# Two-layer feed-forward kernel on TensorE: y operands of layer 2 prepared for two pairs at once, 1024 columns wide

## The chip, the cores and the metric

The kernel runs on one core of a Trainium2 chip. The metric is the time of one execution on the device in microseconds (us), of which the median over several runs is compared.

## The reference

Three stages follow each other on the same 3072 tokens (4 batches x 768):

```python
x = attention(q, k, v, mem_k, mem_v)       # chunked, 8 heads of 64, to (3072, 512)
h = x @ w_in;  x = (h - tanh(h)) @ w_out   # layer 1: 512 -> 2048 -> 512
h = x @ w_in2                              # layer 2: 512 -> 2048
g = maximum(h, 0) + alpha * minimum(h, 0)
out = g @ w_out2                           # y: 2048 -> 512
```

The change touches layer 2 alone.

## The kernel before, in words

Each fp32 operand of a matmul is held as a rounded part (hi) and the rest (lo); a product of two such operands is three matmuls, hi hi, hi lo and lo hi (the table `PASS`). ScalarE (ACT) makes hi by a copy into the rounded type, and VectorE (DVE) or GpSimd (POOL) makes lo = value - hi.

Layer 2 takes both its matmuls in the form with seven block products in place of eight. It goes through the tokens in NB = 3 blocks of 1024 (two halves of 512 columns), and through the 2048 inner channels in P2 = 8 pairs of 256 (two tiles of 128). A block has two stages:

- `pair_h` computes the inner activations of a pair: seven products of six matmuls (L408), numbered 1 to 7, sums of them on DVE (L425, with ACT copies `hs`, `hv`), and `prelu` (ACT L416, L417, DVE L418). It leaves four tiles of 128 x 512: `ga0`, `ga1`, `gb0`, `gb1`, which lie in the pair's `gx` = (ga0, gb1) and `gy` = (ga1, gb0). POOL then makes t3 = gb1 - ga1 (L459) and, in place, ga1 = ga1 - ga0 (L460).
- the y stage goes through the seven products in the order `ORDER` = 1, 6, 5, 2, 7, 3, 4, each a phase of 8 pairs. For a pair, `prep` makes the operand (hi and lo in one tile `go`) and `y_product` issues six matmuls (L502), three for each of two output tiles `yb` in PSUM, which sum over the pairs. `y_done` (L509, L520) combines the products, and L532 turns the result for the store.

The operand of product 1 is ga0, of 5 ga1, of 2 gb0, of 7 t3, of 3 gb1. Product 6 takes t3 + ga0, which L478 writes into a PSUM bank of its own; L481 rounds it, L483 splits it, and L485 puts gb0 minus it over ga0, which is the operand of product 4.

In the main loop `prep` runs LEAD = 6 pairs ahead of `y_product`; EARLY = 4 of them are issued ahead of the block's last pair. Which engine splits: POOL for product 1 from the third pair on, and for every fourth pair of products 5, 2, 7, 3, 4; DVE otherwise. The last pair of a block, the y stage and the first products of the next block are one stream on PE: a scheduler of the Tile framework sets the order on each engine from its own estimate of times, and `issue_after` only moves a piece's priority. In phases 2 to 6, `load_x2`, `sum_x2` (L384) and `split_x2` (L121 on ACT, L122 on POOL) prepare the next block's inputs. SP issues all loads: `wi` (input weights, L370) and `wo` (output weights, L362). The pool `w` of 34 buffers holds `gx`, `gy`, `go` and the weights.

Of the kernel before, what the change touches and what calls it, by code (L numbers as in the profile page):

```python
# [7 lines left out]
FP32 = mybir.dt.float32  # L8
FP32R = mybir.dt.float32r
U32 = mybir.dt.uint32  # L10
U64 = mybir.dt.uint64
ACTF = mybir.ActivationFunctionType
ALU = mybir.AluOpType
# [24 lines left out]
def chunk_attention_two_ffn_kernel(  # L38
# [12 lines left out]
    nc = tc.nc  # L51
# [14 lines left out]
    def f32(ap):  # L66
        return ap.bitcast(FP32)

    const = ctx.enter_context(tc.tile_pool(name="const", bufs=1))
    w_p = ctx.enter_context(tc.tile_pool(name="w", bufs=2 * NF + 2))  # L70
# [274 lines left out]
    P2 = NF // 2  # L345
    NB = NTILE // 8
    NO = 7 * P2 // 2
    LEAD = 6
    EARLY = 4
    wo2 = {}  # L350
    win = {}
    xop = {}
    xin = {}
    gx = {}
    gy = {}
    t3 = {}
    gop = {}

# [42 lines left out]
    def product(h, i, m, first):  # L401
        b = i // P2
        s = WSLOT[m]
        w, x = win[i, s // 2][:, :, s % 2], xop[b, m]
        j = 0
        for kt in range(2):
            for a, c in PASS:
                nc.tensor.matmul(  # L408
                    out=h, lhsT=w[:, a, 128 * kt:128 * kt + 128], rhs=x[c][:, kt, :],
                    start=(first and j == 0), stop=(j == 5), skip_group_check=True,  # L410
                )
                j += 1

    def prelu(t, h, f):
        n = t_p.tile([128, 512], FP32, tag="t", name="n")
        nc.scalar.activation(out=n, in_=h, func=ACTF.Relu, scale=-1.0)  # L416
        nc.scalar.activation(out=n, in_=n, func=ACTF.Copy, scale=alpha_neg[:, f:f + 1])  # L417
        last["pre"] = nc.vector.scalar_tensor_tensor(  # L418
            out=t, in0=h, scalar=0.0, in1=n, op0=ALU.max, op1=ALU.add
        ).ins  # L420

    def pair_h(i):
        b, p = divmod(i, P2)
        f = 2 * p
        add = lambda o, p, q: nc.vector.tensor_tensor(out=o, in0=p, in1=q, op=ALU.add)  # L425
        d = {}
        x = gx[b, p] = w_p.tile([128, 2, 512], FP32, tag="w", name="gx")
        y = gy[b, p] = w_p.tile([128, 2, 512], FP32, tag="w", name="gy")
        if p % 2 == 0:
            t3[b, p // 2] = zr.tile([128, 2, 512], FP32, tag="t3", name="t3")  # L430
        d3 = t3[b, p // 2][:, p % 2]
        ga, gb = (x[:, 0], y[:, 0]), (y[:, 1], x[:, 1])

        for m in (1, 6, 5, 7) if p % 2 else (6, 1, 5, 7):
            if b % 2:
                d[m] = ps_y.tile([128, 512], FP32, tag="y", name="h2")
            elif m in (1, 6):
                d[m] = ps_h.tile([128, 512], FP32, tag="h", name="h2")
            else:
                d[m] = ps_h2.tile([128, 512], FP32, tag="h2", name="h2")  # L440
        product(d[1], i, 1, True)
        hs = g_p.tile([128, 512], FP32, tag="gh", name="hs")
        nc.scalar.activation(out=hs, in_=d[1], func=ACTF.Copy)
        product(d[6], i, 6, True)
        hu = g_p.tile([128, 512], FP32, tag="gl", name="hu")
        add(hu, d[6], hs)
        product(d[5], i, 5, True)
        add(d[5], d[5], hu)
        hv = g_p.tile([128, 512], FP32, tag="gh", name="hv")
        nc.scalar.activation(out=hv, in_=d[5], func=ACTF.Copy)  # L450
        product(d[7], i, 7, True)
        add(gb[1], d[7], hv)
        add(d[7], d[7], hu)
        prelu(gb[1], gb[1], f + 1)
        product(d[1], i, 2, False)
        prelu(ga[0], d[1], f)
        product(d[5], i, 3, False)
        prelu(ga[1], d[5], f)
        nc.gpsimd.tensor_tensor(out=d3, in0=gb[1], in1=ga[1], op=ALU.subtract)  # L459
        nc.gpsimd.tensor_tensor(out=ga[1], in0=ga[1], in1=ga[0], op=ALU.subtract)  # L460
        product(d[7], i, 4, False)
        prelu(gb[0], d[7], f + 1)

    def y_bank(b, m):
        if (b % 2 == 0) == (m in (1, 6)):
            return ps_y.tile([128, 512], FP32, tag="y", name="yb")
        if m in (1, 5):
            return ps_h.tile([128, 512], FP32, tag="h", name="yb")
        return ps_h2.tile([128, 512], FP32, tag="h2", name="yb")

    def prep(b, s):
        mi, p = divmod(s, P2)
        m = ORDER[mi]
        x, y, d3 = gx[b, p], gy[b, p], t3[b, p // 2][:, p % 2]
        op = w_p.tile([128, 2, 512], FP32R, tag="w", name="go")
        if m == 6:
            src = y_bank(b, 7)
            nc.vector.tensor_tensor(out=src, in0=d3, in1=x[:, 0], op=ALU.add)  # L478
        else:
            src = {1: x[:, 0], 5: y[:, 0], 2: y[:, 1], 7: d3, 3: x[:, 1], 4: x[:, 0]}[m]  # L480
        nc.scalar.activation(out=op[:, 0], in_=src, func=ACTF.Copy)  # L481
        eng = nc.gpsimd if (m == 1 and p > 1) or (m not in (1, 6) and p % 4 == 3) else nc.vector
        eng.tensor_tensor(out=op[:, 1], in0=src, in1=f32(op[:, 0]), op=ALU.subtract)  # L483
        if m == 6:
            nc.vector.tensor_tensor(out=x[:, 0], in0=y[:, 1], in1=src, op=ALU.subtract)  # L485
        gop[b, s] = op

    yd = {}
    ye = {}

    def y_product(b, s, tiles=(0, 1)):
        mi, p = divmod(s, P2)
        m = ORDER[mi]
        into = {2: 1, 3: 5, 4: 7}.get(m, m)
        if m == into and p == 0 and 0 in tiles:
            yd[b, m] = [y_bank(b, m) for _ in range(2)]
        w = wo2[b * NO + mi * (P2 // 2) + p // 2][:, p % 2]
        w = w.rearrange("k a (i n) -> k a i n", i=2)
        op = gop[b, s]
        for i in tiles:  # L500
            for n, (a, c) in enumerate(PASS):
                nc.tensor.matmul(  # L502
                    out=yd[b, into][i], lhsT=w[:, a, i], rhs=op[:, c],
                    start=(m == into and p == 0 and n == 0), stop=(p == P2 - 1 and n == 2),
                    skip_group_check=True,
                )
# [224 lines left out]
    if True:  # L731
# [8 lines left out]
        def more_w():  # L740
# [10 lines left out]
            out=ident, in_=ident, compare_op=ALU.not_equal, fill=1.0, base=0,  # L751
# [39 lines left out]
        g = 1e9  # L791
        for t in reversed(range(n0 + 2, NTILE + 1)):
            g = min(base[first_of[t - 1][0]] - 3, g - (per(g) if t < NTILE else 0))
# [3 lines left out]
        for t in range(n0 + 1, NTILE + 1):  # L797
            if t == n0 + 1:
                pos = 2
            else:  # L800
                lo = max(pos + SPACE, release(t - 1))
# [5 lines left out]
        for t in range(n0 + 1, NTILE + 1):  # L807
            a, nxt = at[t], at.get(t + 1, 1e9)
# [15 lines left out]
        for i, (l, b, n, f) in enumerate(slots):  # L824
# [13 lines left out]
            if b == N1 - 1:  # L838
                if f == 0:
                    astack.close()  # L840
                    with tc.issue_after(last["dve"]):
                        nc.vector.tensor_scalar(
                            out=alpha_neg, in0=alpha_sb, scalar1=-1.0, scalar2=None, op0=ALU.mult
# [26 lines left out]
        for b in range(NB):  # L870
            more = b + 1 < NB
            for p in range(P2):
                i = b * P2 + p
                if p == P2 - 1:
                    for s in range(EARLY):
                        prep(b, s)
                if i > 0:
                    pair_h(i)
                for q in range(4):
                    win.pop((i, q))  # L880
                if p + 2 < P2:
                    for q in range(4):
                        load_in(i + 2, q)
            early, late = [], []
            if more:
                work = x2_work(b + 1)
                early, late = work[:8], work[8:]
                late[3:3] = [lambda q=q: load_in((b + 1) * P2, q) for q in range(4)]
                late += [lambda q=q: load_in((b + 1) * P2 + 1, q) for q in range(4)]
            with tc.issue_after(last["pre"]):  # L890
                for s in range(EARLY, LEAD):
                    prep(b, s)
            for s in range(7 * P2):
                if s + LEAD < 7 * P2:
                    with tc.issue_after(last["pre"]):
                        prep(b, s + LEAD)
                if more or s < 6 * P2:
                    y_product(b, s)
                    if s % P2 == P2 - 1:
                        y_done(b, ORDER[s // P2])  # L900
                    i = b * NO + s // 2 + 4
                    if s % 2 and i < NB * NO:
                        load_out(i)
                if s >= 2 * P2 and s % 2 == 0 and early:
                    early.pop(0)()
                if s >= 4 * P2 and late:
                    late.pop(0)()
            if not more:
                for i in range(2):
                    for p in range(P2):  # L910
                        y_product(b, 6 * P2 + p, (i,))
                    y_done(b, 4, (i,))
# [61 lines left out]
```

## Time and profile before

| what | value |
|---|---|
| three runs | 1093.62 us median (1093.38 to 1095.15) |
| profiled execution, its own time | 1096.97 us |
| its span, first to last instruction | 1094.1 us |
| mean granted TensorE clock | 0.992 of full |
| PE, DVE, ACT, POOL busy | 97%, 62%, 49%, 42% |
| matmuls | 6912, of them 1008 at L502 and 1008 at L408 |

Layer 2 begins at about 560 us of the span. Its three y stages begin at about 691, 848 and 1006 us. Line numbers in the rows are those of the kernel before; those of the changed kernel are one or three lines off: L417 there is L418 here, L424 is L425, L458 and L459 are L459 and L460, and L476, L478, L482, L485 are the new lines of `prep`.

### The profile page before, as it was taken

How to read it: one execution, taken by the hardware profiler on the slowest of the kernel's cores; microseconds unless marked ns; L12 is line 12 of the kernel's file. 1: busy time of each engine (PE TensorE's matmuls, PEld its weight loads, DVE VectorE, ACT ScalarE, POOL GpSimd, SP SyncE). 2: the span in 40 equal slices, each digit the busy share in tenths (PEclk: the TensorE clock that was granted, in tenths of full speed). 3: DMA queues.
4: the chain of work that ended last, by engine and by line, in shares of the span. 5: the costliest groups of instructions: out<-in, count | busy, mean ns of one | idle time of the engine just before them, and what ended most of it. 6: DMA issues, size and time to landing. Idle time of an engine off the chain costs nothing. (4 is left out here: it accounts for less than half of the span.)

```text
span 1094.1 us, 18216 instructions
## 1 busy us (share of the span) xinstructions
PE 1056.4 (97%) x6912; PEld 863.4 (79%) x6912; DVE 677.7 (62%) x1087; ACT 535.2 (49%) x956; POOL 464.3 (42%) x351
## 2 busy tenths in 40 slices
PE   4599999999999999999999999999999899999998
PEld 4478878888888888888888888878888688888786
DVE  3688855665776566576321255799555898456873
ACT  3466644444445444454342355655356564465650
POOL 3166634444454453445382122528222467124440
PEclk9699999999999999999999999999999999999999
DMA  9773143554555464454711355488844588833576
GB/s 269 276 259 127 59 145 123 203 168 168 179 184 181 156 204 164 174 174 150 221 32 36 145 176 199 131 265 271 259 170 148 181 248 277 244 135 138 153 213 170
DMA packets 99366, 196.22 MB, mean 179 GB/s; under 512 B 36560, under 2 KB 50896, under 8 KB 99280
## 3 DMA queue, kind: packets, MB, share of 16 engines
q1 hardware_dynamic: 93712, 188.52, 52.6%
q10 hardware_dynamic: 5568, 6.56, 1.7%
q8 instruction: 54, 0.88, 0.3%
q14 instruction: 32, 0.26, 0.1%
HBM read 153.10 MB, written 41.94 MB: 178 GB/s over the span
## 5 line engine op out<-in xcount | busy, mean ns | idle before, releaser
L274 PE MATMUL h<-ring,wt 128*128 128x512 f32 x1152 | 282.6, 393 | 5.9 <-ACT ring L681 2.4
L274 PEld LDWEIGHTS h<-ring,wt 128*128 128x128 f32 x1152 | 217.2, 189 | 52.7 <-ACT ring L681 2.6
L502 PE MATMUL yb<-go,wo 128*128 128x512 f32 x1008 | 235.5, 392 | 5.8 <-DVE go L483 2.7
L502 PEld LDWEIGHTS yb<-go,wo 128*128 128x128 f32 x1008 | 187.9, 188 | 51.1 <-DVE go L483 5.3
L408 PE MATMUL h<-xh,wi 128*128 128x512 f32 x672 | 212.1, 391 | 0.7 <-DVE gx L418 0.4
L299 POOL TENSOR_TENSOR gl<-t,gh 128x512 fp32r<-128x512 f32 x96 | 127.0, 1325 | 173.3 <-ACT gh L298 150.6
L313 PE MATMUL y<-gh,wt 128*128 128x512 f32 x768 | 192.8, 392 | 0.0
L313 PEld LDWEIGHTS y<-gh,wt 128*128 128x128 f32 x768 | 143.2, 188 | 30.4
L290 DVE TENSOR_TENSOR t<-h,t 128x512 f32<-128x512 f32 x96 | 65.9, 687 | 140.8 <-ACT t L289 140.6
L408 PEld LDWEIGHTS h<-xh,wi 128*128 128x128 f32 x672 | 126.2, 188 | 30.6 <-ACT hv L450 2.9
L289 ACT ACTIVATE t<-h 128x512 f32<-128x512 f32 x96 | 56.8, 592 | 112.2 <-PE h L274 92.8
L459 POOL TENSOR_TENSOR t<-gx,gy 128x512 f32<-128x512 f32 x24 | 31.1, 1295 | 175.1 <-DVE gy L418 175.1
L313 PE MATMUL y<-gl,wt 128*128 128x512 f32 x384 | 104.3, 390 | 0.0
L298 ACT ACTIVATE gh<-t 128x512 fp32r<-128x512 f32 x96 | 60.4, 629 | 54.2 <-DVE t L290 47.7
L313 PEld LDWEIGHTS y<-gl,wt 128*128 128x128 f32 x384 | 72.0, 188 | 15.0
L408 PE MATMUL h<-xl,wi 128*128 128x512 f32 x192 | 74.8, 390 | 0.0
L122 POOL TENSOR_TENSOR ws<-sm,ws 128x512 fp32r<-128x512 f32 x32 | 42.8, 1338 | 56.9 <-ACT ws L121 41.4
L417 ACT ACTIVATE n<-n,alpha_neg 128x512 f32<-128x512 f32 x96 | 65.9, 719 | 0.6
L122 POOL TENSOR_TENSOR wt<-s,wt 128x512 fp32r<-128x512 f32 x32 | 41.3, 1294 | 41.0 <-ACT wt L121 39.3
L483 DVE TENSOR_TENSOR go<-gx,go 128x512 fp32r<-128x512 f32 x42 | 57.3, 1406 | 1.4 <-ACT go L481 1.4
L408 PE MATMUL h<-x,wi 128*128 128x512 f32 x144 | 56.1, 390 | 0.0
L483 POOL TENSOR_TENSOR go<-gx,go 128x512 fp32r<-128x512 f32 x30 | 44.0, 1479 | 20.0 <-ACT go L481 20.0
(95 smaller groups left out, 1364.5 us busy)
## 6 DMA issues: line engine op xcount, KB each, us to landing
wo<-w2o SPq DMA_DIRECT2D x84, 512.0 KB, 4.2
wi<-w2i SPq DMA_DIRECT2D x72, 512.0 KB, 4.9
kn<-in_k_dram SPq DMA_DIRECT2D x24, 384.0 KB, 4.5
vn<-in_v_dram SPq DMA_DIRECT2D x24, 384.0 KB, 3.8
ri<-in_moe_w_in_dram SPq DMA_DIRECT2D x16, 512.0 KB, 7.7
ro<-in_moe_w_out_dram SPq DMA_DIRECT2D x16, 512.0 KB, 8.5
pk<-in_moe_w_in_dram SPq DMA_DIRECT2D x16, 512.0 KB, 4.0
pk<-in_moe_w_out_dram SPq DMA_DIRECT2D x16, 512.0 KB, 4.1
```

The lines of the kernel that those rows point to most:

```text
L122: nc.gpsimd.tensor_tensor(out=lo, in0=v, in1=f32(hi), op=ALU.subtract)
L274: last["ffn"] = nc.tensor.matmul(out=h, lhsT=wi[:, a, kk, :], rhs=ring[c][:, s0:s0 + n, kk, :], start=(i == 0), stop=(i == 3 * KD - 1),).ins
L289: nc.scalar.activation(out=t, in_=h, func=ACTF.Tanh)
L290: last["dve"] = nc.vector.tensor_tensor(out=t, in0=h, in1=t, op=ALU.subtract).ins
L298: nc.scalar.activation(out=gh, in_=t, func=ACTF.Copy)
L299: nc.gpsimd.tensor_tensor(out=gl, in0=t, in1=f32(gh), op=ALU.subtract)
L313: mm = nc.tensor.matmul(out=yp[l, b][j][:, :n * 128], lhsT=wo[:, a, j * 128:(j + 1) * 128], rhs=g[c], start=first, stop=final,)
L408: nc.tensor.matmul(out=h, lhsT=w[:, a, 128 * kt:128 * kt + 128], rhs=x[c][:, kt, :], start=(first and j == 0), stop=(j == 5), skip_group_c ...
L417: nc.scalar.activation(out=n, in_=n, func=ACTF.Copy, scale=alpha_neg[:, f:f + 1])
L459: nc.gpsimd.tensor_tensor(out=d3, in0=gb[1], in1=ga[1], op=ALU.subtract)
L483: eng.tensor_tensor(out=op[:, 1], in0=src, in1=f32(op[:, 0]), op=ALU.subtract)
L502: nc.tensor.matmul(out=yd[b, into][i], lhsT=w[:, a, i], rhs=op[:, c], start=(m == into and p == 0 and n == 0), stop=(p == P2 - 1 and n == ...
```

## The change

- The four activations become four tiles of 128 x 2 x 512, one for each two pairs (`gq`), in place of `gx` and `gy` of each pair.
- `prep` works on two pairs at once: one rounding and one split, each 1024 columns, into two tiles, `goh` and `gol`.
- The sum for product 6 is made in place in SBUF over ga0 (L476), not in a PSUM bank; the operand of product 4 is made in place over gb0 (L478), in product 4's own phase, not in product 6's.
- LEAD and EARLY are counted in double pairs: 3 and 2.
- POOL splits product 1 for three of four double pairs, and the last double pair of the other products in the last block only.

The number of matmuls and what they multiply stay the same.

```diff
     P2 = NF // 2
     NB = NTILE // 8
     NO = 7 * P2 // 2
-    LEAD = 6
-    EARLY = 4
+    LEAD = 3
+    EARLY = 2
...
-        x = gx[b, p] = w_p.tile([128, 2, 512], FP32, tag="w", name="gx")
-        y = gy[b, p] = w_p.tile([128, 2, 512], FP32, tag="w", name="gy")
         if p % 2 == 0:
+            for n in ("ga0", "ga1", "gb0", "gb1"):
+                gq[b, n, p // 2] = w_p.tile([128, 2, 512], FP32, tag="w", name=n)
             t3[b, p // 2] = zr.tile([128, 2, 512], FP32, tag="t3", name="t3")
         d3 = t3[b, p // 2][:, p % 2]
-        ga, gb = (x[:, 0], y[:, 0]), (y[:, 1], x[:, 1])
+        ga, gb = [[gq[b, f"g{r}{k}", p // 2][:, p % 2] for k in range(2)] for r in "ab"]
...
     def prep(b, s):
-        mi, p = divmod(s, P2)
+        mi, pp = divmod(s, P2 // 2)
         m = ORDER[mi]
-        x, y, d3 = gx[b, p], gy[b, p], t3[b, p // 2][:, p % 2]
-        op = w_p.tile([128, 2, 512], FP32R, tag="w", name="go")
+        ga0, ga1, gb0, gb1 = [gq[b, n, pp] for n in ("ga0", "ga1", "gb0", "gb1")]
+        d3 = t3[b, pp]
         if m == 6:
-            src = y_bank(b, 7)
-            nc.vector.tensor_tensor(out=src, in0=d3, in1=x[:, 0], op=ALU.add)
-        else:
-            src = {1: x[:, 0], 5: y[:, 0], 2: y[:, 1], 7: d3, 3: x[:, 1], 4: x[:, 0]}[m]
-        nc.scalar.activation(out=op[:, 0], in_=src, func=ACTF.Copy)
-        eng = nc.gpsimd if (m == 1 and p > 1) or (m not in (1, 6) and p % 4 == 3) else nc.vector
-        eng.tensor_tensor(out=op[:, 1], in0=src, in1=f32(op[:, 0]), op=ALU.subtract)
-        if m == 6:
-            nc.vector.tensor_tensor(out=x[:, 0], in0=y[:, 1], in1=src, op=ALU.subtract)
-        gop[b, s] = op
+            nc.vector.tensor_tensor(out=ga0, in0=d3, in1=ga0, op=ALU.add)
+        if m == 4:
+            nc.vector.tensor_tensor(out=gb0, in0=gb0, in1=ga0, op=ALU.subtract)
+        src = {1: ga0, 6: ga0, 5: ga1, 2: gb0, 7: d3, 3: gb1, 4: gb0}[m]
+        hi = w_p.tile([128, 2, 512], FP32R, tag="w", name="goh")
+        lo = w_p.tile([128, 2, 512], FP32R, tag="w", name="gol")
+        nc.scalar.activation(out=hi, in_=src, func=ACTF.Copy)
+        pool = pp > 0 if m == 1 else b == NB - 1 and pp == 3
+        eng = nc.gpsimd if pool else nc.vector
+        eng.tensor_tensor(out=lo, in0=src, in1=f32(hi), op=ALU.subtract)
+        gop[b, s] = hi, lo
...
-        op = gop[b, s]
+        op = gop[b, s // 2]
...
-                    out=yd[b, into][i], lhsT=w[:, a, i], rhs=op[:, c],
+                    out=yd[b, into][i], lhsT=w[:, a, i], rhs=op[c][:, p % 2],
...
-                if s + LEAD < 7 * P2:
+                if s % 2 == 0 and s // 2 + LEAD < NO:
                     with tc.issue_after(last["pre"]):
-                        prep(b, s + LEAD)
+                        prep(b, s // 2 + LEAD)
```

The change moves instructions on DVE and POOL where a block's y stage begins. DVE in the kernel before, from the activations of the block's last pair (L418) to the second double pair of product 6 in block 0; `t_6408` and `t_6606` are t3 of the first two double pairs, `yb` the PSUM bank:

```order
L418 SCALAR_TENSOR_TENSOR gx<-gx,n 128x512
L418 SCALAR_TENSOR_TENSOR gx<-h_7028,n 128x512
L418 SCALAR_TENSOR_TENSOR gy<-h_7030,n 128x512
L418 SCALAR_TENSOR_TENSOR gy<-h_7031,n 128x512
L478 TENSOR_TENSOR yb<-t_6408,gx 128x512 x2
L483 TENSOR_TENSOR go<-yb,go 128x512
L485 TENSOR_TENSOR gx<-gy,yb 128x512
L483 TENSOR_TENSOR go<-yb,go 128x512
L485 TENSOR_TENSOR gx<-gy,yb 128x512
L478 TENSOR_TENSOR yb<-t_6606,gx 128x512 x2
```

The same place in the changed kernel; `ga_6406`, `ga_6604`, `ga_6771`, `ga_6938` are ga0 of the four double pairs, `gb_6941` and `gb_6940` gb1 and gb0 of the last, `ga_6939` its ga1:

```order
L417 SCALAR_TENSOR_TENSOR gb_6941<-gb_6941,n 128x512
L417 SCALAR_TENSOR_TENSOR ga_6938<-h_7024,n 128x512
L417 SCALAR_TENSOR_TENSOR ga_6939<-h_7026,n 128x512
L417 SCALAR_TENSOR_TENSOR gb_6940<-h_7027,n 128x512
L476 TENSOR_TENSOR ga_6406<-t_6410,ga_6406 128x1024
L476 TENSOR_TENSOR ga_6604<-t_6608,ga_6604 128x1024
L476 TENSOR_TENSOR ga_6771<-t_6775,ga_6771 128x1024
L476 TENSOR_TENSOR ga_6938<-t_6942,ga_6938 128x1024
L485 TENSOR_TENSOR gol<-ga_6406,goh 128x1024
L485 TENSOR_TENSOR gol<-ga_6604,goh 128x1024
L485 TENSOR_TENSOR gol<-ga_6771,goh 128x1024
L485 TENSOR_TENSOR gol<-ga_6938,goh 128x1024
```

The four sums for product 6 now stand together ahead of the four splits, where sums, splits and the sums for product 4 took turns.

POOL in the kernel before, at the same place; `go<-gx` are the splits of product 1, L459 and L460 of `t_6940` belong to the last double pair, its first and then its second pair:

```order
L459 TENSOR_TENSOR t_6940<-gx,gy 128x512
L460 TENSOR_TENSOR gy<-gy,gx 128x512
L483 TENSOR_TENSOR go<-gx,go 128x512 x3
L459 TENSOR_TENSOR t_6940<-gx,gy 128x512
L483 TENSOR_TENSOR go<-gx,go 128x512 x3
L460 TENSOR_TENSOR gy<-gy,gx 128x512
```

POOL in the changed kernel:

```order
L458 TENSOR_TENSOR t_6942<-gb_6941,ga_6939 128x512
L459 TENSOR_TENSOR ga_6939<-ga_6939,ga_6938 128x512
L485 TENSOR_TENSOR gol<-ga_6604,goh 128x1024
L485 TENSOR_TENSOR gol<-ga_6771,goh 128x1024
L485 TENSOR_TENSOR gol<-ga_6938,goh 128x1024
L458 TENSOR_TENSOR t_6942<-gb_6941,ga_6939 128x512
L459 TENSOR_TENSOR ga_6939<-ga_6939,ga_6938 128x512
L122 TENSOR_TENSOR x_7293<-x_7293,xh 128x1024
```

The second pair's difference of t3 now stands behind all splits of product 1, not between them, and the third of these reads what the last pair writes.

## Rows read from the trace of the kernel before

**Rows 1.** The page, part 1: busy us (share of the span) and instructions of each engine.

```profile
PE 1056.4 (97%) x6912; PEld 863.4 (79%) x6912; DVE 677.7 (62%) x1087; ACT 535.2 (49%) x956; POOL 464.3 (42%) x351
```

**Rows 2.** Waits of PE: us in total, times, longest us.

```profile
PE yb L502 <- DVE go L483: 2.7, 2, 1.6
...
PE yb L502 <- ACT go L481: 1.8, 5, 0.4
...
PE yb L502 <- POOL go L483: 1.2, 3, 0.4
```

**Rows 3.** Busy us (count) by stretch: PE, PEld, DVE, ACT, POOL, clock, DMA share, GB/s.

```profile
755.00:780.00 25.00, 25.00 (x112) 20.71 (x111) 18.03 (x20) 7.80 (x12) 13.06 (x7) 1.00 0.75 240
695.00:755.00 60.00, 58.52 (x252) 46.53 (x251) 54.11 (x63) 36.08 (x62) 29.73 (x18) 1.00 0.75 242
850.00:915.00 65.00, 61.78 (x268) 49.52 (x267) 57.92 (x68) 38.90 (x65) 40.80 (x21) 1.00 0.75 239
1010.00:1040.00 30.00, 28.93 (x122) 22.27 (x122) 25.27 (x37) 20.46 (x38) 13.60 (x10) 1.00 0.50 148
```

**Rows 4.** Timeline of PE, blocks 0 and 1: start, us, instruction, count [idle before <-releaser].

```profile
691.57 0.62 PE L502 MATMUL yb<-go,wo 128*128 128x512 f32 x2
...
703.46 9.40 PE L502 MATMUL yb<-go,wo 128*128 128x512 f32 x40 [0.40 <-POOL go L483]
...
866.08 6.16 PE L502 MATMUL yb<-go,wo 128*128 128x512 f32 x24 [1.65 <-DVE go L483]
873.27 1.90 PE L502 MATMUL yb<-go,wo 128*128 128x512 f32 x7 [1.04 <-DVE go L483]
```

**Rows 5.** Operations by form, ns min/median/max; last, a load (KB, us to landing).

```profile
L481 ACT ACTIVATE go<-gx x72: 613/620/636, 689.4 to 1060.5; 128x512 fp32r<-128x512 f32 x72
L121 ACT ACTIVATE xh<-x x9: 1039/1055/1065, 549.0 to 912.7; 128x1024 fp32r<-128x1024 f32 x9
L384 DVE TENSOR_TENSOR xt<-x,x x6: 1212/1214/1226, 540.2 to 891.9; 128x1024 f32<-128x1024 f32 x6
L122 POOL TENSOR_TENSOR x<-x,xh x9: 2388/2410/2862, 550.1 to 916.2; 128x1024 fp32r<-128x1024 f32 x9
L418 DVE SCALAR_TENSOR_TENSOR gx<-gx,n x24: 691/693/694, 626.5 to 1011.9; 128x512 f32<-128x512 f32 x24
wi<-w2i SPq DMA_DIRECT2D x72, 512.0 KB, 4.9
```

**Rows 6.** Timeline of DVE and POOL, block 0, and POOL in block 1.

```profile
689.70 1.29 POOL L459 TENSOR_TENSOR t<-gx,gy 128x512 f32<-128x512 f32 x1 [7.84 <-DVE gy L418]
...
690.15 1.39 DVE L483 TENSOR_TENSOR go<-gx,go 128x512 fp32r<-128x512 f32 x1
...
691.07 1.62 POOL L460 TENSOR_TENSOR gy<-gy,gx 128x512 f32<-128x512 f32 x1
...
702.37 0.69 DVE L418 SCALAR_TENSOR_TENSOR gy<-h,n 128x512 f32<-128x512 f32 x1 [2.63 <-ACT n L417]
702.98 2.68 DVE L478 TENSOR_TENSOR yb<-t,gx 128x512 f32<-128x512 f32 x2
...
706.76 1.30 POOL L460 TENSOR_TENSOR gy<-gy,gx 128x512 f32<-128x512 f32 x1
706.77 0.68 DVE L483 TENSOR_TENSOR go<-yb,go 128x512 fp32r<-128x512 f32 x1
...
888.08 7.43 POOL L483 TENSOR_TENSOR go<-t,go 128x512 fp32r<-128x512 f32 x1 [4.90 <-ACT go L481]
```

**Rows 7.** Clock: timeline of PE at 28 to 33 us, and two stretches.

```profile
28.44 0.22 PE L661 MATMUL tp<-marks,sc 128*32 128x64 f32 x1
32.91 0.54 PE L661 MATMUL tp<-marks,sc 128*32 128x64 f32 x7 [4.11 <-issue]
...
31.00:38.00 7.00, 5.09 (x101) 4.46 (x103) 1.06 (x3) 1.18 (x2) 1.04 (x1) 0.51 0.90 362
...
862.00:868.00 6.00, 4.35 (x18) 3.04 (x17) 6.00 (x8) 2.77 (x5) 2.87 (x2) 1.00 0.56 175
```

More of the change, by code (lines that the diff above doesn't have):

```diff
@@ L353, in chunk_attention_two_ffn_kernel @@
     xin = {}
-    gx = {}
-    gy = {}
+    gq = {}
     t3 = {}
```

## The prediction

> **What bounds the kernel now.** I read the page's busy shares first: TensorE (PE) is busy for 97% of the span [rows 1], so a gain can come only from its idle time, and a loss only from new idle time or a lower clock. Next the waits of PE in the layer that the change touches: the second matmul waits for its rounded and split operands, for DVE 2.7 us, ACT 1.8 and POOL 1.2 [rows 2]. These sums hide part, because matmuls overlap. So I read PE's rate from the busy times by stretch [rows 3]. A matmul lasts 0.39 us, and the first and last of a window are counted though partly outside, 1.7 too many in all. In 755 to 780 us, where nothing waits, 112 - 1.7 = 110.3 matmuls take 25.00 us: **0.2267 us each**. By that pace the starts of the three blocks lose: 60 - 250.3 x 0.2267 = 3.3 us, 65 - 266.3 x 0.2267 = 4.6 us, 30 - 120.3 x 0.2267 = 2.7 us, together **10.6 us**. This is the most that better operands can win. The timeline of PE shows where it goes [rows 4]: at 703.46 PE waits for a POOL split of product 1, at 866.08 (1.65 us) and 873.27 (1.04 us) for DVE splits of product 6. The sum at L478, the round at L481, the split at L483 and the next sum at L485 are a chain on DVE there.
>
> The profiled execution took 1096.97 us with a span of 1094.1; the median of the three runs is 1093.62, 3.35 less. The sum below is a difference against that execution, and I add it to the median. Some 0.2%, 2.2 us, is what a measurement can tell from no change.
>
> **The change part by part.**
>
> *Width.* ACT's 168 roundings of 512 columns (0.62 us) become 84 of 1024 (nearest row 1.055 us, L121); DVE's and POOL's 168 splits become 84 (DVE 1.21 us by L384, POOL 2.41 us by L122 [rows 5]). One phase of the loop gives PE 12 matmuls per two pairs, 2.72 us. DVE instructions in a row start 0.08 us before the one ahead ends (702.37 and 702.98 [rows 6]), so a wide one takes 1.13 us; a split and a sum, 2.26 us, stay below PE's, so in mid-block the new operands are hidden by PE: nothing gained, nothing lost. If that cover were gone, each pair of operands would cost what it is late, as below. The moved sum of product 4 (now in its own phase) goes beside PE in the same way. The price of width is latency: the first pair's operand is ready only when both are.
>
> *Product 6 in place, at a block's start.* Before, the four sums stand in pieces between splits and read or write a PSUM bank; now four wide sums (L476) stand in a row on DVE, the splits of product 6 behind all of them, and the last sum overwrites `ga0` of pair 7, so it follows POOL's L458, L459 of pair 7. On POOL these two now stand behind three wide splits of product 1, while before three narrow ones went ahead of L459.
>
> What DVE and POOL do to each other I take from the trace [rows 6]. At 690.15 a DVE split with both inputs in SBUF lasts 1.39 us, not 0.68, while POOL's L459 runs until 690.99; L460, which then starts at 691.07, lasts 1.62 instead of 1.29, ending 1.15 us behind DVE's split. So they exclude each other. At 706.77 a DVE split that reads PSUM (`go<-yb`) takes 0.68 us beside POOL's L460: no exclusion. The change turns the second kind into the first. Whether L417 on `gb1` (L418 before, `gx<-gx,n`, two SBUF inputs, 24 of about 0.69 us [rows 5]) also waits, no row shows, since POOL is idle beside it. From below it costs 0, from above one POOL split, 2.41 us. I take the wait: its inputs are those of the split at 690.15, the nearest row.
>
> The Trainium skill, SBUF — State Buffer, section Who interferes with whom, says that a DVE instruction with two SBUF inputs contends with a GpSimd instruction that reads SBUF, and the second to issue is fully blocked. The rows at 690.15 and 691.07 agree; for L417 none shows it; by the rule my forecast stands, and without it the time of the second rival follows.
>
> *Laid out for block 0.* PE starts product 7 of pair 7 at 691.57, where two y matmuls stood [rows 4]. Up to the first matmul with a split operand of product 6 it has 18 matmuls of products 7, 3, 4, the 48 of product 1 and 2 more: 68 x 0.2267 us later, **706.98**. On DVE the first wide split follows `hu` directly, 691.01 to 692.22. On POOL: L459 of pair 6 runs until 693.37 (1.15 behind that split, as L460 above), then the splits of double pairs 1 and 2 (2.38 each, 2.41 less a small overlap) until 698.13. L417 on `gb1`, ready at 696 (behind `hv` and its two ACT steps), waits for that and ends 698.68 (plus 0.55, the end of the split at 690.15 behind POOL), L417 on `ga0` 699.29, ACT's wide round 700.37, POOL's third split 702.81, L458 704.07. DVE's last L417 ends at 703.06 as before [rows 6], because PE's product 4 sets it. The four sums and L459 then alternate: 4 x 1.13 + 1.25 = 5.8, ending 709.8; the first split of product 6 another 1.13: **710.95**. PE stands **4.0 us**. Nothing before or behind it in the phase should be late (product 1's splits are ready by 702.8, wanted at 704.3). All three blocks have this order: 3 x 3.97 = 11.9 us lost against 10.6: **+1.3 us**.
>
> *The clock behind the stall.* At 32.91 PE had been idle 4.11 us and the granted clock fell: 0.51 from 31 to 38 us. Behind the gap that ended at 866.08 it stayed 1.00 [rows 7]. The new stall is nearest to the first row. Such a stretch of 7 us at half speed costs at most 3.4 us, at least 0 (PE was also idle in it); I take half, 1.7 us. The three stalls lie between the two rows, so I count two falls of three: **+3.4 us**. At two of three the ends are 0 and 6.8.
>
> *SP's queue.* Loads of `wi` and `wo` shift against each other: in blocks 1 and 2 a `wi` load of the fourth pair goes ahead of those of the third, waiting on a product of PE. A load takes 4.9 us to land [rows 5] and is wanted some 5.4 us behind its release: 0, at most 0.5 us each.
>
> *POOL late in blocks 0 and 1.* The splits L122 of the next block meet more wide DVE operations; a narrow POOL split was starved to 7.43 us at 888.08 [rows 6]. The x operands are wanted a phase later: 0, at most 1.5 us.
>
> Sum: -10.6 + 11.9 + 3.4 = **+4.7 us: 1098.3 us**.
>
> **Rivals.**
> 1. *The chain feeds PE in time (faster).* If DVE gets its sums in without waiting for POOL, the floor is 703.06 + 4 x 1.13 + 1.13 = 708.7, a stall of 1.73 us per block, too short for the clock (the gap ending at 866.08). 5.2 - 10.6 = -5.4: **1088.2 us**. It decides if L459 of pair 7 ends by 706.4, so that the fourth sum isn't held. For it: POOL's rows are rough, and DVE starved POOL at 888.08. Against: three wide splits and L458, L459 are 9.8 us of POOL work from 693.37 without any wait, which ends at 703.2 only if none is delayed.
> 2. *L417 isn't held by POOL.* Then the round of double pair 3 ends at 699.25, POOL's split 701.7, L458 and L459 704.2, sums 708.7, split 709.8: a stall of 2.85. 8.55 - 10.6 = -2.1: **1091.6 us**, within 0.2%, or 1095.0 with two clock falls. For it: no row shows L417 waiting.
> 3. *The clock holds*, stalls as forecast: +1.3, **1094.9 us**. For it: the clock held behind 1.65 us of idling; against: 4 us is not that.
> 4. *Loads or L122 late* on top of the forecast: +1 to +2.5 more, **1099 to 1101 us**.
>
> That the change doesn't do what it says would leave 1093.6; the order of instructions rules that out.
>
> **How the numbers follow.** Forecast 0.38, rival 1 0.24, rival 2 0.20, rival 3 0.10, rival 4 0.08. Faster by over 0.2%: rival 1 and 0.06 of rival 2, 0.30. Within: rival 3 and 0.12 of rival 2, 0.22. Slower: forecast, rival 4, 0.02 of rival 2: 0.48. The forecast's own range is 1094.9 (no fall) to 1101.7 (two at 3.4). The range for all reaches down just below rival 1, 1087.5, and up to 1102.
>
> **What would show it.** Right: in PE's waits one idle piece of about 4 us per block, some 15.5 us behind the start of product 7 of pair 7, ended by DVE L485; no waits of product 1 on POOL; L476 x4 in a row lasting about 6 us with POOL's L459 among them; L417 on `gb1` far longer than 0.69 us; a granted clock below 1.00 just behind. Rival 1 shows as stalls below 2 us. The forecast is wrong if PE waits somewhere else, as for `wi`, or if the stalls are as long and the time lower: then the 10.6 us were mis-sized.

## The result and the profile after

The changed kernel took **1106.58 us** (median of five runs, 1106.24 to 1110.99), the kernel before 1095.1 us in the same comparison (1093.38 to 1096.25, five runs): a ratio of 1.0119, interval 1.0104 to 1.0135, so 11 to 15 us slower. The two medians lie 11.5 us apart, at the lower end of that. The forecast was slower by 4.7 us, 1098.3, with a range that ended at 1102. The sign was right and the size too small.

The profiled execution took 1110.99 us with a span of 1109.1, 15.0 us more than the span before. Some 1.6 us of that lie ahead of layer 2, whose first matmul starts at 593.1 us (591.5 before). From there to the start of the last matmul it takes 511.0 us, 497.5 before: 13.4 us more. First the waits of PE in layer 2 of the changed kernel (us in total, times, longest), which answer to [rows 2]:

```profile
PE yb L502 <- DVE gol L485: 11.3, 3, 3.8
PE h L407 <- DMA wi<-w2i: 1.9, 1, 1.9
```

The small waits on POOL and ACT are gone. In place of many stand three, one per block, of up to 3.8 us, and one on a weight load, which the kernel before didn't have. Next its busy times in the 50 us that hold each block's start, and in two short stretches (columns as in [rows 3]; the first figure behind the POOL column is the granted clock):

```profile
690.00:740.00 50.00, 46.28 (x194) 37.75 (x193) 42.76 (x41) 30.18 (x39) 14.15 (x7) 0.93 0.59 191
850.00:900.00 50.00, 46.23 (x193) 37.70 (x192) 42.80 (x41) 30.32 (x39) 14.15 (x7) 0.93 0.59 189
1010.00:1060.00 50.00, 46.23 (x192) 37.65 (x191) 42.80 (x36) 30.25 (x39) 23.74 (x10) 0.93 0.36 108
638.00:644.00 6.00, 5.34 (x17) 4.25 (x17) 2.39 (x4) 3.53 (x6) 0.00 (x0) 0.72 1.04 410
716.00:722.00 6.00, 5.70 (x14) 4.50 (x15) 6.00 (x7) 6.00 (x7) 0.00 (x0) 0.54 0.09 8
```

With the prediction's reckoning (count less 1.7, times 0.2267 us) the three blocks lose 50 - 192.3 x 0.2267 = 6.4, 6.6 and 6.9 us, together **19.9 us** against 10.6 before. Behind the stalls the clock is 0.54: near its lower level, 1.2 GHz.

The timeline of the chain in block 0, DVE first, then POOL, then PE (start, us, instruction, count, idle before):

```profile
701.42 2.67 DVE L417 SCALAR_TENSOR_TENSOR gb<-gb,n 128x512 f32<-128x512 f32 x1 [1.19 <-ACT n L416]
...
707.87 0.69 DVE L417 SCALAR_TENSOR_TENSOR gb<-h,n 128x512 f32<-128x512 f32 x1 [0.75 <-ACT n L416]
708.48 6.63 DVE L476 TENSOR_TENSOR ga<-t,ga 128x1024 f32<-128x1024 f32 x4
715.03 3.48 DVE L485 TENSOR_TENSOR gol<-ga,goh 128x1024 fp32r<-128x1024 f32 x3
```

```profile
698.78 4.76 POOL L485 TENSOR_TENSOR gol<-ga,goh 128x1024 fp32r<-128x1024 f32 x2
705.86 2.40 POOL L485 TENSOR_TENSOR gol<-ga,goh 128x1024 fp32r<-128x1024 f32 x1 [2.32 <-ACT goh L482]
708.23 1.29 POOL L458 TENSOR_TENSOR t<-gb,ga 128x512 f32<-128x512 f32 x1
709.60 2.16 POOL L459 TENSOR_TENSOR ga<-ga,ga 128x512 f32<-128x512 f32 x1
```

```profile
711.73 0.85 PE L502 MATMUL yb<-goh,wo 128*128 128x512 f32 x3
716.30 0.79 PE L502 MATMUL yb<-gol,wo 128*128 128x512 f32 x1 [3.72 <-DVE gol L485]
716.89 0.63 PE L502 MATMUL yb<-goh,wo 128*128 128x512 f32 x1
717.32 0.63 PE L502 MATMUL yb<-gol,wo 128*128 128x512 f32 x1
...
721.56 0.39 PE L502 MATMUL yb<-gol,wo 128*128 128x512 f32 x1
721.78 0.39 PE L502 MATMUL yb<-goh,wo 128*128 128x512 f32 x1
```

L417 on `gb1` starts at 701.42 and ends 0.55 us behind the end of POOL's two splits, 703.54. The four sums take 6.63 us, with POOL's L459 (2.16 us, not 1.29) among them. PE's last matmul before the stall starts at 712.19 and the next is due at 712.41; it comes at 716.30, **3.9 us** late. From there to 721.56 matmuls start 0.43 us apart, not 0.2267: of this block's 6.4 us, 2.5 us go to the clock. The stalls of the other two blocks are as long, so of the 19.9 us the clock takes 8.2, **2.7 us** per block.

The weight load of block 0, on PE and on SP's queue of the changed kernel:

```profile
636.38 0.39 PE L407 MATMUL h<-xh,wi 128*128 128x512 f32 x1
638.66 0.47 PE L407 MATMUL h<-xh,wi 128*128 128x512 f32 x1 [1.90 <-DMA wi<-w2i]
```

```profile
615.95 1.75 SPq L361 DMA_DIRECT2D wo<-w2o  x4
632.72 12.25 SPq L369 DMA_DIRECT2D wi<-w2i  x8
```

SP's queue in the kernel before:

```profile
614.72 1.37 SPq L362 DMA_DIRECT2D wo<-w2o  x3
616.13 23.46 SPq L370 DMA_DIRECT2D wi<-w2i  x8
```

The loads of the third pair went out at 616 us before and at 632.72 now, since a load of the fourth pair that waits for a product of PE stands ahead of them. That wait is the longest of the `wi` loads from 590 to 700 us, 14.9 us (10.5 in the kernel before):

```profile
SPq L369 <- PE h L407: 64.7, 13, 14.9
```

Between the two matmul starts around PE's wait lie 2.28 us in place of 0.23, and the clock falls behind that too (0.72 in 638 to 644): the thirteen steps from 638.66 to 643.31 take 4.6 us in place of 2.9, another 1.7 us, about **3.8 us** in all. So these terms come to 19.9 - 10.6 + 3.8 = 13.1 us, against the 13.4 that layer 2 took longer. The four other executions had spans of 1104.5 to 1105.0 and a mean clock of 0.984, against 0.981 in the profiled one: less of their time was at the lower clock. Which of the falls was shorter or missing in them, no trace shows.

### The profile page after: what moved, and what is told of

Its sections match the earlier page's. It is cut to its first block, busy times and chain, and to the rows that moved or that the text cites. A ratio compares the mean times of both kernels' runs of the same rounds, so it can differ in the third digit from the quotient of the medians.

```text
span 1109.1 us, 17928 instructions
## 1 busy us (share of the span) xinstructions
PE 1063.1 (96%) x6912; PEld 870.9 (79%) x6912; DVE 659.0 (59%) x1012; ACT 526.7 (47%) x872; POOL 428.8 (39%) x318
## 4 chain that ended last, share of the span: by engine, by line
PE 89%; DVE 4%; DMA 3%; issue 2%; ACT 1%; SPq 0%; POOL 0%; ACTq 0%; POOLq 0%; DVEq 0%
PE h L274 23%; PE y L313 23%; PE yb L502 20%; PE h L407 20%; PE pv L674 2%; DVE ga L476 2%; PE sp L590 2%; DMA y1d<-ys 1%; DMA qn<-in_q_dram 1%; PE tp L661 1%; DVE h L424 1%; DMA wi<-w2i 0%; ACT hv L449 0%; DVE gol L485 0%; DVE u L108 0%
## 5 line engine op out<-in xcount | busy, mean ns | idle before, releaser
L407 PE MATMUL h<-xh,wi 128*128 128x512 f32 x672 | 213.0, 393 | 2.4 <-DMA wi<-w2i 1.9
L502 PE MATMUL yb<-goh,wo 128*128 128x512 f32 x672 | 213.2, 398 | 0.0
L407 PEld LDWEIGHTS h<-xh,wi 128*128 128x128 f32 x672 | 127.0, 189 | 33.9 <-ACT hv L449 3.9
L502 PEld LDWEIGHTS yb<-goh,wo 128*128 128x128 f32 x672 | 129.8, 193 | 27.5
L502 PE MATMUL yb<-gol,wo 128*128 128x512 f32 x336 | 134.3, 400 | 11.3 <-DVE gol L485 11.3
L458 POOL TENSOR_TENSOR t<-gb,ga 128x512 f32<-128x512 f32 x24 | 31.2, 1299 | 199.2 <-DVE ga L417 199.2
L502 PEld LDWEIGHTS yb<-gol,wo 128*128 128x128 f32 x336 | 65.1, 194 | 26.3 <-DVE gol L485 12.6
L407 PE MATMUL h<-xl,wi 128*128 128x512 f32 x192 | 74.7, 389 | 0.0
L122 POOL TENSOR_TENSOR ws<-sm,ws 128x512 fp32r<-128x512 f32 x32 | 42.3, 1321 | 59.3 <-ACT ws L121 43.9
L449 ACT ACTIVATE hv<-h 128x512 f32<-128x512 f32 x24 | 14.4, 599 | 94.5 <-DVE h L424 91.0
L122 POOL TENSOR_TENSOR wt<-s,wt 128x512 fp32r<-128x512 f32 x32 | 41.2, 1291 | 41.6 <-ACT wt L121 41.3
```

Source lines behind the costliest of these rows:

```text
L122: nc.gpsimd.tensor_tensor(out=lo, in0=v, in1=f32(hi), op=ALU.subtract)
L407: nc.tensor.matmul(out=h, lhsT=w[:, a, 128 * kt:128 * kt + 128], rhs=x[c][:, kt, :], start=(first and j == 0), stop=(j == 5), skip_group_c ...
L502: nc.tensor.matmul(out=yd[b, into][i], lhsT=w[:, a, i], rhs=op[c][:, p % 2], start=(m == into and p == 0 and n == 0), stop=(p == P2 - 1 an ...
```

## The experiments

The theory: three terms make the loss, in each block a stall by the place of the four sums, the clock behind it, and the load of block 0. Rivals: the width of the operands, and the waits of DVE and POOL for each other alone. Each run was timed against the kernel before on the same chip: 1094.21 us for e2, e4, e6 and e7, 1094.81 for e3, e5, e8 and e9. A difference between two runs below is one of medians, and where the two were timed apart, some 1 us of it can be such a shift.

**e4: PE kept busy in the stall.** The extra matmuls write a bank that product 6's first matmul clears.

```diff
         op = gop[b, s // 2]
+        if m == 6 and p == 0:
+            for k in range(16):
+                nc.tensor.matmul(
+                    out=yd[b, 6][0], lhsT=w[:, 0, 0], rhs=gop[b, P2 // 2 - 1][0][:, 1],
+                    start=True, stop=True, skip_group_check=True,
+                )
         for i in tiles:
```

> The changed kernel with 16 extra matmuls per block at the start of product 6, into a bank that its first real matmul clears again; they take 16 x 0.2267 = 3.6 us, about as long as the stall of 3.9 us, so that PE stays busy while it waits. Theory (behind each stall the granted clock falls and costs 2.9 us): the stall's end doesn't move, the clock stays 1.00 in the y stages, 3 x 2.9 = 8.6 us less than the changed kernel: 1097 to 1099 us. Rival (the clock costs nothing, the slow matmuls are hidden by DVE that is late anyway): 1106 to 1107 us.

Measured: 1100.1 us (1099.84 to 1100.57), ratio 1.0044, interval 1.0028 to 1.0061: 6.5 us less than the changed kernel, though PE does 48 matmuls more. Its busy times at the blocks' starts:

```profile
684.00:734.00 50.00, 49.91 (x220) 40.96 (x220) 42.07 (x42) 31.10 (x40) 14.13 (x7) 1.00 0.58 193
842.00:892.00 50.00, 49.54 (x218) 40.38 (x217) 42.25 (x41) 30.96 (x40) 14.14 (x7) 1.00 0.59 193
1001.00:1051.00 50.00, 49.85 (x220) 40.97 (x219) 42.80 (x36) 30.25 (x39) 23.85 (x10) 1.00 0.38 118
```

The clock holds. The blocks lose 0.5, 1.0 and 0.5 us, and the 48 extra matmuls take 10.9: 12.9 us against 19.9, 7.0 less. That is less than the expected 8.6, as these 12.9 us are 1.2 over three stalls of 3.9. The operands are no earlier here: in block 0 the first split of product 6 ends 19.2 us behind the start of the last pair's product 7, as in the changed kernel. Only the clock is kept. The clock's term is thus shown: 6.5 us with the filling's excess, near 8 without.

**e2: the wide operands without the sums in place.**

```diff
-        if m == 6:
-            nc.vector.tensor_tensor(out=ga0, in0=d3, in1=ga0, op=ALU.add)
-        if m == 4:
-            nc.vector.tensor_tensor(out=gb0, in0=gb0, in1=ga0, op=ALU.subtract)
-        src = {1: ga0, 6: ga0, 5: ga1, 2: gb0, 7: d3, 3: gb1, 4: gb0}[m]
         hi = w_p.tile([128, 2, 512], FP32R, tag="w", name="goh")
         lo = w_p.tile([128, 2, 512], FP32R, tag="w", name="gol")
+        if m == 6:
+            for k in range(2):
+                src = y_bank(b, 7)
+                nc.vector.tensor_tensor(out=src, in0=d3[:, k], in1=ga0[:, k], op=ALU.add)
+                nc.scalar.activation(out=hi[:, k], in_=src, func=ACTF.Copy)
+                nc.vector.tensor_tensor(out=lo[:, k], in0=src, in1=f32(hi[:, k]), op=ALU.subtract)
+                nc.vector.tensor_tensor(out=ga0[:, k], in0=gb0[:, k], in1=src, op=ALU.subtract)
+            gop[b, s] = hi, lo
+            return
+        src = {1: ga0, 5: ga1, 2: gb0, 7: d3, 3: gb1, 4: ga0}[m]
```

> Wide operands, but the sums for products 6 and 4 as in the kernel before: narrow, in a PSUM bank, alternating with the splits; the rest of the change stays. Theory (the row of four wide sums ahead of the first split of product 6 costs a 3.9 us stall and a clock fall of about 2.9 us per block): both go; DVE's chain of sum, split and sum, 1.8 us against PE's 1.36 per pair, is back, as is some 3 us per block of small waits, and the late wi load of block 0 stays: 1094 to 1099 us, no clock below 1.00 in the y stages. Rival (the width itself, two pairs for one operand, makes product 1 and 6 late): 1104 us or more, with waits on gol of product 1 too.

Measured: 1097.32 us (1095.81 to 1098.51, ten runs), ratio 1.0024, interval 1.0015 to 1.0034. PE's waits in layer 2:

```profile
PE yb L507 <- ACT goh L481: 2.8, 6, 0.5
PE yb L507 <- DVE gol L482: 2.1, 2, 1.1
PE h L407 <- DMA wi<-w2i: 2.1, 1, 2.1
```

The stalls are gone and the small waits of before are back; no wait is on product 1. What is left over the kernel before, 3.1 us by the medians, is in the main the load: layer 2 takes 2.2 us longer from its first matmul to its last. The width by itself costs nothing that shows.

**e3: the sums in place without the width**, as an edit of the kernel before.

```diff
         if m == 6:
-            src = y_bank(b, 7)
-            nc.vector.tensor_tensor(out=src, in0=d3, in1=x[:, 0], op=ALU.add)
-        else:
-            src = {1: x[:, 0], 5: y[:, 0], 2: y[:, 1], 7: d3, 3: x[:, 1], 4: x[:, 0]}[m]
+            nc.vector.tensor_tensor(out=x[:, 0], in0=d3, in1=x[:, 0], op=ALU.add)
+        if m == 4:
+            nc.vector.tensor_tensor(out=y[:, 1], in0=y[:, 1], in1=x[:, 0], op=ALU.subtract)
+        src = {1: x[:, 0], 6: x[:, 0], 5: y[:, 0], 2: y[:, 1], 7: d3, 3: x[:, 1], 4: y[:, 1]}[m]
...
-        if m == 6:
-            nc.vector.tensor_tensor(out=x[:, 0], in0=y[:, 1], in1=src, op=ALU.subtract)
         gop[b, s] = op
```

> The kernel before with one part of the change alone: the sums for products 6 and 4 in place in SBUF, the latter in its own phase; operands stay one pair and 512 columns wide. In its order DVE has six narrow sums in a row ahead of the first split of product 6, against POOL's three narrow splits and L460. Theory (the row of sums with SBUF inputs, excluded by POOL, is what stalls PE, narrow or wide): a stall of 2 to 5 us per block with a clock fall behind it, 1096 to 1106 us. Rival (width is what costs): no stall above 2 us, within 0.2% of the kernel before or faster, 1090 to 1096 us.

Measured: 1101.58 us (1100.25 to 1102.19), ratio 1.0061, interval 1.0043 to 1.0078. DVE in block 0, and the waits of PE on DVE:

```profile
701.27 7.26 DVE L477 TENSOR_TENSOR gx<-t,gx 128x512 f32<-128x512 f32 x6
708.46 0.68 DVE L483 TENSOR_TENSOR go<-gx,go 128x512 fp32r<-128x512 f32 x1
```

```profile
PE yb L500 <- DVE go L483: 8.5, 3, 2.8
```

Six narrow sums in a row last 7.26 us (alone 6 x 0.6 = 3.6; the rest is waiting for POOL), the first split comes behind them, and PE stalls once per block. So it is the row of sums with SBUF inputs, drawn out by POOL, that stalls PE, narrow or wide. The two parts weigh differently: here POOL adds some 3.7 us to the row, more than the stall, while in the changed kernel it adds 6.63 - 4 x 1.13 = 2.1 us, about half of one. No run has such a row with POOL idle.

**e6: the loads in order by pair**, an edit of priority alone.

```diff
-        nc.sync.dma_start(
+        last["in"] = nc.sync.dma_start(
             out=f32(w).rearrange("p a s n -> p (a s n)"),
-            in_=w2i[p][:, 1024 * q:1024 * q + 512 * n])
+            in_=w2i[p][:, 1024 * q:1024 * q + 512 * n]).ins
...
-                    for q in range(4):
-                        load_in(i + 2, q)
+                    with tc.issue_after(last["in"]):
+                        for q in range(4):
+                            load_in(i + 2, q)
```

> The changed kernel with the loads of input weights tied to their order by pair (priority alone), so that the third pair's loads in block 0 no longer stand behind a load of the fourth pair that waits for PE. Theory (the late load costs PE a wait of 1.9 us and a clock fall of 1.9 us in block 0 in the profiled execution, in the timed ones at least the wait): no wait on wi at about 638 us, 2 to 4 us less than the changed kernel: 1102.5 to 1104.5 us. Rival (seen in the profiled execution alone): 1106 to 1107 us. The stalls of 3.9 us at product 6 stay in all three blocks by both.

Measured: 1098.19 us (1097.28 to 1101.05), ratio 1.0034, interval 1.0018 to 1.0049: 8.4 us less than the changed kernel, twice what was expected. The only wait of PE in layer 2 is now:

```profile
PE yb L502 <- DVE gol L485: 11.2, 3, 3.8
```

The load's 3.8 us are gone, the stalls stay. Some 2.5 us more came from what the edit moved besides, ACT's order in the pairs, and with it small waits on `hv` at L407: in 790 to 850 and 950 to 1010 us PE starts 533 matmuls here and 522 in the changed kernel. Another 2.0 us came from the clock, behind stalls that are as long:

```profile
690.00:740.00 50.00, 46.28 (x198) 37.85 (x197) 41.00 (x37) 27.76 (x34) 13.12 (x7) 0.97 0.66 215
850.00:900.00 50.00, 46.24 (x193) 37.67 (x192) 39.89 (x35) 26.88 (x32) 13.64 (x8) 0.93 0.65 207
1010.00:1060.00 50.00, 46.24 (x197) 37.74 (x196) 39.98 (x31) 29.45 (x35) 22.01 (x9) 0.97 0.52 158
```

By the count these blocks lose 5.5, 6.6 and 5.7 us, 17.9 in place of 19.9. Less 3.9 for the stall, the fall cost 1.6, 2.7 and 1.8 us.

**e8: the same edit on the kernel before** (e6's diff, at the same lines of the kernel before).

> The kernel before with e6's edit of the loads' priority alone; PE, DVE and POOL keep their order, ACT's order in the pairs changes with it. Theory (in e6 the edit won 4 us from the late wi load of block 0, which the kernel before doesn't have, and some 2.7 us from small waits on hv at L408, by ACT's order): 2 to 3.5 us less than the kernel before, 1090.5 to 1092.5 us, with L408's small waits gone. Rival (the loads cost the kernel before as much, 7 to 8 us): 1086 to 1088 us.

Measured: 1092.87 us (1091.08 to 1094.62, ten runs), ratio 0.9981, interval 0.9971 to 0.9990: 1.9 us less than the kernel before, a little less than expected. The pairs from 780 to 850 us, in e8 and then in the kernel before:

```profile
780.00:850.00 70.00, 70.00 (x311) 57.95 (x310) 39.71 (x59) 43.02 (x76) 21.45 (x16) 1.00 0.58 185
```

```profile
780.00:850.00 70.00, 69.88 (x307) 56.98 (x307) 39.43 (x59) 41.85 (x73) 19.36 (x15) 1.00 0.55 182
```

311 matmuls in place of 307: the small waits on `hv` are what it wins there. The kernel before did not pay for the loads; the changed one did.

**e7: the sums ahead of the last pair**, on top of e6.

```diff
-                    for s in range(EARLY):
+                    for s in (0, 1, 2, 4, 5):
                         prep(b, s)
...
-                for s in range(EARLY, LEAD):
+                for s in (3, 6):
                     prep(b, s)
...
-                if s % 2 == 0 and s // 2 + LEAD < NO:
+                if s % 2 == 0 and s // 2 + LEAD < NO and (b, s // 2 + LEAD) not in gop:
...
-        pool = pp > 0 if m == 1 else b == NB - 1 and pp == 3
+        pool = 0 < pp < 3 if m == 1 else b == NB - 1 and pp == 3
```

> On top of e6: the operands of product 6 for the first two double pairs are issued ahead of the block's last pair, right behind product 1's for the first three, and the fourth split of product 1 goes to DVE, so that POOL has two wide splits, then L458 and L459. Theory (what is lost is the place of the four sums, not their width or being in place): the first split of product 6 is ready before PE wants it, no stall above 1 us in the y stages, no clock fall: the 10.5 us of waits before are won, 1082 to 1088 us. Rival (width, or DVE and POOL excluding each other, is what costs): stalls move to product 1 or to the products of the last pair, 1094 us or more.

Measured: **1082.2 us** (1081.5 to 1082.86), ratio 0.9880, interval 0.9865 to 0.9894: faster than both kernels. Its blocks' starts, and DVE there:

```profile
690.00:740.00 50.00, 50.00 (x222) 41.39 (x222) 46.34 (x43) 28.48 (x36) 13.56 (x7) 1.00 0.72 231
850.00:900.00 50.00, 50.00 (x223) 41.39 (x222) 47.42 (x41) 28.77 (x33) 12.92 (x6) 1.00 0.77 257
1010.00:1060.00 50.00, 50.00 (x223) 41.39 (x222) 41.77 (x35) 23.23 (x26) 18.05 (x7) 1.00 0.68 204
```

```profile
694.78 3.41 DVE L476 TENSOR_TENSOR ga<-t,ga 128x1024 f32<-128x1024 f32 x1 [1.09 <-POOL gol L485]
698.11 1.21 DVE L485 TENSOR_TENSOR gol<-ga,goh 128x1024 fp32r<-128x1024 f32 x1
...
700.45 1.21 DVE L485 TENSOR_TENSOR gol<-ga,goh 128x1024 fp32r<-128x1024 f32 x1
```

PE has no wait in layer 2, and the three windows lose nothing by the count. The operands are as wide, the sums as much in place, and DVE still waits for POOL (the sum at 694.78 takes 3.41 us, not 1.21), but the first two splits of product 6 are done by 701.7, before PE wants them. e7 differs from the changed kernel in three things: the loads' order, which is e6, one split moved from POOL to DVE, which is e5's edit, and the place of the sums. The stalls stay in e6 and in e5 and go here, so that loss was in the order of the sums.

**e9: the early sums without e6's edit** (e7's diff, on the changed kernel).

> e7 without e6's edit of the loads: the changed kernel, with product 6's first two operands issued ahead of the last pair and the fourth split of product 1 on DVE. Theory (two separate losses, the place of the sums and the late load): no stall in the y stages, the wait on wi at about 638 us with its clock fall and the small waits on hv stay, 6 to 8 us above e7: 1088 to 1090.5 us. Rival (the early sums only help with the loads in order): stalls in the y stages again, 1095 us or more.

Measured: 1087.38 us (1086.64 to 1087.68), ratio 0.9934, interval 0.9915 to 0.9953, 5.2 us above e7 and a little below the expected span. In layer 2 PE's one listed wait is the load:

```profile
PE h L407 <- DMA wi<-w2i: 1.9, 1, 1.9
```

So the place of the sums and the load are two losses, each on its own.

**e5: e6 with POOL relieved of one split.** This tells the row of sums from POOL's third split.

```diff
-        pool = pp > 0 if m == 1 else b == NB - 1 and pp == 3
+        pool = 0 < pp < 3 if m == 1 else b == NB - 1 and pp == 3
```

> e6 with the fourth split of product 1 on DVE in place of POOL, so that L458 and L459 of the last pair come one wide POOL split (2.4 us) earlier; the four sums keep their place behind the activations. Theory (the four sums and this split stand in a row on DVE, 5 x 1.13 us plus the first split, behind an end of the activations that PE sets): the stall stays 3 to 4 us, the clock falls, 1096 to 1099 us. Rival (POOL's third split, and DVE's wait for it, is what holds the chain): stall below 2 us, no clock fall, 1087 to 1091 us.

Measured: 1101.38 us (1098.24 to 1102.3), ratio 1.0054, interval 1.0037 to 1.0072. Its waits of PE, and DVE in block 0:

```profile
PE yb L502 <- DVE gol L485: 8.1, 3, 2.7
PE yb L502 <- ACT goh L482: 2.3, 3, 0.8
```

```profile
702.30 0.69 DVE L417 SCALAR_TENSOR_TENSOR gb<-h,n 128x512 f32<-128x512 f32 x1 [0.77 <-ACT n L416]
702.90 1.22 DVE L485 TENSOR_TENSOR gol<-ga,goh 128x1024 fp32r<-128x1024 f32 x1
704.04 5.71 DVE L476 TENSOR_TENSOR ga<-t,ga 128x1024 f32<-128x1024 f32 x4
```

The stalls stay, 2.7 + 0.8 us per block: what POOL no longer holds, DVE's own row does. The median is above the expected span; PE reaches the first stall 2.6 us later than in e6, and from its first matmul to its last layer 2 takes 502.6 us in e5 and 502.4 in e6. So in the profiled executions the difference arose ahead of layer 2, in stages that no edit touches, and isn't explained.

## Why the prediction was right and wrong

- **Product 6 at a block's start: right, to a tenth.** Counted from the start of the last pair's product 7 (691.57 in the layout; six matmuls ahead of 698.35 in the trace, 696.99), L417 on `gb1` was to end at +7.11 and ended at +7.10; POOL's third split +11.24 and +11.27; the row of sums +18.2 and +18.1. The stall was to be 3.97 us and was 3.9, in all three blocks: 11.7 us for 11.9.
- **L417 waits for POOL: right.** 2.67 us where 24 of them took 0.69 [rows 5]. The Trainium skill, SBUF — State Buffer, section Who interferes with whom, has a DVE instruction with two SBUF inputs blocked by a GpSimd one that started first; the 2.67 us agree. The second rival, without this wait, falls.
- **The waits before: right.** 10.6 us by the count; e7, without any, shows that they could be won: it took 10.7 us less than e8, the kernel before with its loads in order too.
- **The clock behind the stall: this step failed in its size.** It counted two falls of three at 1.7 us, 3.4 us. In the changed kernel's trace the clock fell in all three blocks, and a fall cost 2.7 us: 8.2 us. e4, where only the clock is kept, confirms the term. The price was halved since PE idled in the row used, 31 to 38 us [rows 7]; here PE had matmuls waiting from the end of the stall until the clock rose. The count failed in every run with stalls: in e3, e5 and e6 too the clock fell in all three blocks. The price of 1.7 us did not fail in every one: in e6, behind the same stalls, it was met in two blocks of three.
- **SP's queue: this step failed too.** It looked for the load of the fourth pair ahead of the third's in blocks 1 and 2 and gave it 0, at most 0.5 us each. It also stands so in block 0, where the load waited 14.9 us in SP's queue for a product; the third pair's loads went out 16 us later than before, and PE lost about 3.8 us, wait and clock, in the profiled execution. The prediction had named a wait on `wi` as a sign that it was wrong.
- **Width and POOL late: right at nothing.** e2 and e7 show no price of the width, and no wait on the next block's x operands appears.
- **Rivals.** The first (the chain feeds PE in time) falls for this order: the stalls were 3.9 us, not 1.73. The sign that it gave did not decide: POOL's L459 of the last pair ended at +14.8, as early as it asked (706.4, +14.8), but POOL had held the first two sums (2.12 and 2.32 us in place of 1.21). In e7, with another order, the chain does feed PE in time. The third (the clock holds) is refuted by the rows at 0.93. The fourth named late loads, at 1 to 2.5 us with L122; the load of block 0 alone cost 3.8.

With the terms of the profiled execution the prediction's sum is -10.6 + 11.7 + 8.2 + 3.8 = 13.1 us. The ratio gives 13.0 (1.0119 x 1095.1 - 1095.1) and the medians 11.5; as the profiled execution is the longest of the five, some of its falls may be dearer than in the others. Of the 8.3 us between forecast and measured time 1.5 are the base: the forecast was added to 1093.62, and the kernel before took 1095.1 in the comparison. Why the scheduler put the fourth pair's load ahead in block 0 was not tried.

## What to carry to other kernels

Where a wide form of a chain (sums, rounds, splits) replaces a narrow one that took turns, look at what stands ahead of the first result on its in-order engine: the same work, with two operands issued earlier, one split moved and the loads in order, took 12 us less than the kernel before, where the change took some 12 more. A stall of PE is to be priced with the slow clock behind it, which here added 1.6 to 2.9 us to stalls of 3.9. And when only one stage is edited, compare the order of every queue over the whole program: a load that had passed another, far ahead of the edit, cost as much as one stall.

## What the runs showed that was not expected

Gaps of about the same length between matmul starts end differently. In block 0 the wait on `wi` made a gap of 2.28 us in the changed kernel and of 2.26 us in e9; the granted clock fell behind the first (0.72 in the rows above) and held behind the second:

```profile
635.00:641.00 6.00, 5.40 (x24) 4.49 (x25) 2.31 (x4) 4.42 (x8) 0.00 (x0) 1.00 1.04 410
```

24 matmuls in 6 us there, 17 in the changed kernel. At the same place a gap of 2.32 us in e4 brought a fall (0.72 in 634 to 640) and one of 2.47 in e2, the longest of the four, brought none (1.00 in 636 to 642). The gaps of e3 (3.24 us), e5 (3.11, close behind one of 1.15), e6 (4.11 to 4.16) and the changed kernel (4.11 to 4.16) all brought a fall; those of the kernel before (2.04 at most in layer 2) did not. Nor is the price fixed: behind the equal stalls of e6 a fall cost 1.6, 2.7 and 1.8 us, and 2.5, 2.7 and 2.9 in the changed kernel. So neither whether a gap of 2.3 us slows PE nor what a fall costs can be read from the gap's length alone.
